# All of one float64 weight matrix narrowed beside the first batch's spectra, and the second batch's last spectra ordered behind routing steps

## Chip, cores and metric

The kernel runs on one core of a Trainium2 chip. The metric is device time in microseconds (us) of one execution; lower is better. The engines are TensorE (PE, matrix products; PEld is its load of stationary weights), VectorE (DVE), ScalarE (ACT), GpSimdE (POOL) and SyncE (SP, which issues most DMAs). Each engine takes its instructions strictly in the order in which the program was built, so an instruction that waits holds up everything behind it on that engine.

## What is computed

The reference has three steps on x of shape (4, 3072, 256), cut here to its core:

```python
X = np.fft.rfft(x, axis=1)
Yr = Xr @ w_r - Xi @ w_i + b_r
Yi = Xr @ w_i + Xi @ w_r + b_i
Yr, Yi = soft_threshold(Yr, 0.01), soft_threshold(Yi, 0.01)
x = np.fft.irfft(Yr + 1j * Yi, n=3072, axis=1).reshape(12288, 256)
logits = x @ w_gate                                     # 8 experts
each token: its best expert, gate weight = softmax there;
the first 384 tokens of each expert are kept
out = gate_w * (relu(x_kept @ w1[e]) @ w2[e]),  0 for the others
h = out @ w_in                                          # 256 x 2048
result = (h * sigmoid(h)) @ w_out                       # 2048 x 256
```

The matrices w_in and w_out of the last step come as float64. A program on this chip has no float64 arithmetic, so the kernel reads their bits as pairs of int32 and makes float32 of them with shifts and masks; this is called narrowing here.

## The kernel before

The kernel keeps float32 accuracy on PE by splitting each operand into a high and a low part and multiplying three times: mm3 (L205, L206, L207) is high x high, high x low and low x high. The high part is a copy into the rounded type by ACT (L189), the low part is the difference, by DVE or POOL (L197).

The kernel needs only the tokens that are kept, and goes on until all experts are full; for these inputs the first two of the four batches do nearly all of it. In the order of time the program does this:

1. `first` (L365): x of batch 0 is fetched in nine transfers on SP (L379, the last is `loads[8]`) and multiplied by a DFT table, in eight strips m with two halves c. Each product of a half goes to one PSUM tile ps of a pool with three buffers; half 0 is evicted to xs by ACT and half 1 by DVE (L387).
2. `kphase(0)` (L410), the spectra of batch 0: for k = 0, 2, ... 22 it turns xs (L428), finishes the DFT (xp, L436), multiplies by the weights (yp, shrink, eight times mm3, so 24 matmuls for a group), thresholds on DVE (L476 to L479, the step tail or y, then cl), and goes back (bp, L485), which ACT evicts to bo (L189) and writes to DRAM as b_d (L488). Beside it run `s1(1)` (L390), the first step of batch 1, `load_tables` (L305) and `ffn_in(0, 4)`.
3. `kphase(1)`, the same for batch 1; it reads ar from DRAM (L420). Beside it: `is2(0)`, which reads b_d back as br (L634), finishes the inverse transform (ps by L361), turns it (tp, L648) and makes the logits (lg, L661; turned back as lt, L668), and `ffn_in(4, 8)`.
4. `route(0)` (L681): the place of each token by running sums on DVE, a sum over the partitions on PE (bs, L695 to L698), one-hot matrices pm (L738 to L741), and the table of the kept tokens (tb, 24 matmuls, L753); then `rank` and `slots` (L767 to L815, DVE and POOL), which give the row numbers srcs.
5. `experts` (L919): for each expert nine rows' blocks are gathered for the first three experts by POOL's indirect DMAs (xg, L1046, three for an expert), scaled (DVE, L1057), turned (gtp, L1064), split to xT, and go through the first product (hp), relu (hh on ACT, hl on DVE) and the second (y). The weights come in quarters st on SP and are split on ACT and on DVE or POOL (w, L189 and L197). Beside experts 0 to 2 run `third(1)` (L560; reads br, L575, L589, L597, L602), `route(1)` and the second `slots`. From the point E in the order of the experts on, `second_ffn` does the last step for pairs of experts; `pair` (L1099) makes the sums t1, t2, m1 to m4 of two experts' results that it multiplies.

One part of w_in (`ffn_part`, L877) is 128 rows x 512 columns of float64. Its narrowing (`narrow`, L853) is one DMA of 512 KB into nt on SP (L861), |high word| on ACT (na, L867), and on DVE a clamp (L868), the sign (nsg, L872) and two shifts (L873, L874). Each part is then split into the weight wi by ACT and POOL; every second part also makes sums mt on DVE (L904 to L907), which are stored (L909). w_out goes the same way in `ffn_out`, one part at each step n in the list AHEAD, all behind routing.

What sets the order: the generators are stepped in turn by `mix`, with the weights of its list; the pools' buffers give the waits; and `self.after(a, b)` keeps a behind b when the instructions are put in order, without a wait at run time. The scheduler then lines up each engine's instructions by its own reckoning of when the data is there. `narrow` puts its DMA behind `self.fetched`, which is the last load of x at first and is moved forward by `kphase`. The DMAs that SP and ACT issue go to the same 16 DMA engines.

## Time and profile before

| | us |
|---|---|
| three runs | 622.52, 624.06, 628.26 |
| median | 624.06 |
| the profiled execution, as timed | 625.83 |
| its span in the trace | 624.0 |
| PE busy in it | 601.4 |
| DVE / ACT / POOL busy | 419.7 / 339.8 / 202.7 |

The profile is of one execution, and its durations are set against that execution's own 625.83 us. Busy means that the engine had an instruction in work; PE's ends are modelled, so overlapping matmuls look longer (0.28 us) than the distance at which they start. In a timeline row the first number is the start in us from the beginning of the span, the second how long the row lasted, then engine, line, operation, what it wrote and read, and how many; the bracket gives the idle time of the engine ahead of it and what ended that.

### The profile page before, as it was taken

Reading aid. Unit: us, or ns where it says so; the run is one execution under the profiler, and the core shown is the slowest. Engines: PE = TensorE matmul, PEld = TensorE weight load, DVE = VectorE, ACT = ScalarE, POOL = GpSimd, SP = SyncE. Lnnn points to the kernel's source line nnn. Section 1 sums busy time; section 2 is a strip of 40 time slices with the busy share of each in tenths; the row PEclk is TensorE's granted clock in tenths of the full one; section 3 lists DMA queues with packets and bytes.
Section 4 is the critical chain, followed back from the end, with each engine's and each line's share of the span. In section 5 each row is a group of like instructions: output and inputs, shape, how many; then the busy total and the mean of one; then the engine's idle time right before and its main releaser. Section 6 shows DMA issues by size and latency. Waiting matters only on the chain. (4 is left out here: it accounts for less than half of the span.)

```text
span 624.0 us, 11502 instructions
## 1 busy us (share of the span) xinstructions
PE 601.4 (96%) x4128; PEld 560.0 (90%) x4128; DVE 419.7 (67%) x837; ACT 339.8 (54%) x722; POOL 202.7 (32%) x196
## 2 busy tenths in 40 slices
PE   9999999799997998999999999999999999999994
PEld 9887898557996778989999999999999999999994
DVE  2454887545884669999876687576587567485563
ACT  2535555343453556457765657556557555465552
POOL 1000113300025324355754503445403343154433
PEclk9999999899998999999999999999999999999998
DMA  8638867894427777810453543413443130010001
GB/s 213 191 94 251 280 207 233 232 270 111 169 80 238 203 226 251 285 53 26 141 186 116 151 135 111 155 32 119 138 128 105 57 128 27 13 65 27 15 3 55
DMA packets 66011, 86.09 MB, mean 138 GB/s; under 512 B 6068, under 2 KB 55864, under 8 KB 65944
## 3 DMA queue, kind: packets, MB, share of 16 engines
q1 hardware_dynamic: 53976, 69.53, 37.1%
q10 hardware_dynamic: 9664, 9.44, 4.9%
q0 software_dynamic: 2304, 6.29, 3.1%
q8 instruction: 34, 0.56, 0.4%
q14 instruction: 33, 0.27, 0.1%
HBM read 54.31 MB, written 30.93 MB: 137 GB/s over the span
## 5 line engine op out<-in xcount | busy, mean ns | idle before, releaser
L1235 DVE TENSOR_TENSOR u<-h,u 128x384 f32<-128x384 f32 x224 | 117.6, 552 | 57.0 <-PE h L207 51.9
L1158 ACT ACTIVATE u<-u 128x384 f32<-128x384 f32 x128 | 64.2, 522 | 71.0 <-DVE u L1235 70.4
L206 PE MATMUL o<-wo,gl 128*128 128x256 f32 x366 | 98.8, 282 | 0.6 <-DVE gl L197 0.6
L207 PE MATMUL o<-wo,gh 128*128 128x256 f32 x366 | 98.9, 282 | 0.0
L205 PE MATMUL o<-wo,gh 128*128 128x256 f32 x366 | 86.8, 282 | 0.1
L197 POOL TENSOR_TENSOR ring<-mt,ring 128x384 fp32r<-128x384 f32 x32 | 37.9, 1186 | 129.4 <-ACT ring L189 129.4
L197 POOL TENSOR_TENSOR gl<-u,gh 128x384 fp32r<-128x384 f32 x62 | 65.1, 1068 | 29.1 <-ACT gh L189 26.4
L206 PEld LDWEIGHTS o<-wo,gl 128*128 128x128 f32 x366 | 69.2, 189 | 1.2 <-DVE gl L197 0.9
L207 PEld LDWEIGHTS o<-wo,gh 128*128 128x128 f32 x366 | 69.0, 189 | 0.0
L189 ACT CAST gh<-u 128x384 fp32r<-128x384 f32 x126 | 63.3, 510 | 5.3 <-PE o L207 3.7
L205 PEld LDWEIGHTS o<-wo,gh 128*128 128x128 f32 x366 | 64.6, 189 | 0.4 <-ACT gh L189 0.4
L205 PE MATMUL yp<-wri,xk 128*128 128x256 f32 x188 | 56.6, 301 | 0.9 <-DVE tail L476 0.9
L1086 ACT ACTIVATE hh<-hp 128x384 fp32r<-128x384 f32 x64 | 31.4, 491 | 46.6 <-PE y L206 23.6
L1087 DVE SCALAR_TENSOR_TENSOR hl<-hp,hh 128x384 fp32r<-128x384 f32 x64 | 35.1, 552 | 29.8 <-ACT hh L1086 26.0
L206 PE MATMUL yp<-wri,xk 128*128 128x256 f32 x188 | 54.5, 290 | 0.0
L207 PE MATMUL yp<-wri,xk 128*128 128x256 f32 x188 | 54.3, 289 | 0.0
L197 DVE TENSOR_TENSOR w<-st,w 128x512 fp32r<-128x512 f32 x52 | 38.1, 741 | 19.2 <-ACT w L189 18.4
L189 ACT CAST w<-st 128x512 fp32r<-128x512 f32 x64 | 38.7, 619 | 16.5 <-DMA st<-in_moe_w 8.9
L205 PE MATMUL hp<-xT,w 128*128 128x384 f32 x128 | 44.1, 345 | 1.6 <-DVE xT L197 1.6
L197 POOL TENSOR_TENSOR wi<-na,wi 128x256 fp32r<-128x256 f32 (+1 forms) x8 | 11.4, 1425 | 100.1 <-ACT wi L189 100.1
L205 PE MATMUL y<-hh,w 128*128 128x384 f32 x128 | 43.5, 340 | 0.0
L206 PE MATMUL hp<-xT,w 128*128 128x384 f32 x128 | 43.4, 339 | 0.0
(254 smaller groups left out, 1544.7 us busy)
## 6 DMA issues: line engine op xcount, KB each, us to landing
st<-in_moe_w SPq DMA_DIRECT2D x64, 256.0 KB, 3.1
out<-zt SPq DMA_DIRECT2D x48, 256.0 KB, 3.2
b_d<-bo ACTq DMA_DIRECT2D x12, 512.0 KB, 4.4
mt<-mixed SPq DMA_DIRECT2D x32, 192.0 KB, 2.4
xt<-in_x SPq DMA_DIRECT2D x15, 384.0 KB, 6.8
nt<-in_moe_w_in SPq DMA_DIRECT2D x8, 512.0 KB, 5.3
nt<-in_moe_w_out SPq DMA_DIRECT2D x16, 256.0 KB, 5.5
a_d<-ao SPq DMA_DIRECT2D x8, 384.0 KB, 4.2
```

The source lines that it names most:

```text
L189: self.lastact = self.nc.scalar.copy(dst, src)
L197: return e.tensor_tensor(dst, src, raw(hi), ALU.subtract).ins
L205: first = nc.tensor.matmul(out, lh, rh, start=start, stop=False)
L206: nc.tensor.matmul(out, ll, rh, start=False, stop=False)
L207: return first.ins, nc.tensor.matmul(out, lh, rl, start=False, stop=stop).ins
L1086: self.rectified = nc.scalar.activation(hh, hp, AF.Relu).ins
L1087: self.evicted = nc.vector.scalar_tensor_tensor(hl, hp, 0.0, raw(hh), ALU.max, ALU.subtract).ins
L1158: act.activation(sg, sg, AF.Silu)
L1235: v.tensor_tensor(to, h, u, ALU.add)
```

## The change

- `ffn_in` takes all eight parts of w_in in the first mix (with the first spectra), with no steps of delay, and none beside the second spectra. Parts 0 and 1 are put right behind the ninth transfer of x (`loads[8]`); the others stay behind `fetched`.
- HOLD: the shrinks of batch 1 for k = 10, 14 and 18 are held behind the last lt of `is2(0)`, the last bs of `route(0)` and the last tb.
- AHEAD, the steps at which parts of w_out are narrowed, goes from 4, 8, 12, 16, 20 to 7, 10, 13, 16, 20.
- `third(1)` starts four steps later and takes 5 + 2n instead of 2 + 2n steps between its parts; its first matmul of each tile is put behind `lasty`, the last product y of an expert that stands before it.
- The low half of the first quarter of expert 0's w2 goes from POOL to DVE.
- `pair`: its tiles m1 to m4 and b2 move from the pool mb to mg, the tiles gh and gl of `second_ffn` from mg to mb, and the first pair's sums are put behind the one-hot matrix of `route(1)` (`self.made`).

The diff, cut to the lines around its edits:

```diff
@@ -35,11 +35,12 @@
 WARM = 11
-AHEAD = 4, 8, 12, 16, 20
+AHEAD = 7, 10, 13, 16, 20
 PMS = "vav"
...
 PACE = {4: 2, 5: 5, **{n: GT - 1 for n in range(6, 12)}}
+HOLD = {10: "lt", 14: "bs", 18: "tb"}
 BIG = 65536.0
@@ -172,6 +173,7 @@
         self.again, self.away, self.evicted, self.gated = False, False, None, {}
+        self.held, self.lasty = {}, None
 
@@ -258,12 +260,13 @@
                 next(g)
-            mix([tables, spectra, self.s1(1, ads), self.ffn_in(0, 4)], [4, 10, 24, 10], lead=[0, 0, 0, 0])
+            mix([tables, spectra, self.s1(1, ads), self.ffn_in(0, 8, 0)], [4, 10, 24, 8], lead=[0, 0, 0, 0])
             rest = self.kphase(1, ads, True)
...
                 self.route_consts()
-            mix([self.is2(0, (0, 1, 2), self.res), self.ffn_in(4, 8)], [10, 7])
+            for _ in self.is2(0, (0, 1, 2), self.res):
+                pass
             self.route(0, (0, 1, 2), self.res)
@@ -470,7 +473,9 @@
                             l = [xk[:, h, 2 * j + c, 64 - 64 * jj:192 - 64 * jj] for h in range(2)]
-                        self.mm3(yp[:, j], l[0], l[1], wri[:, jj, 0, c], wri[:, jj, 1, c], jj + c == 0, jj + c == 2)
+                        ins = self.mm3(yp[:, j], l[0], l[1], wri[:, jj, 0, c], wri[:, jj, 1, c], jj + c == 0, jj + c == 2)[0]
+                        if b == 1 and k in HOLD and not jj and not c:
+                            self.after(ins, self.held[HOLD[k]])
             y = self.spare(1, "y")
@@ -572,7 +577,9 @@
                     u = 2 * w + z
-                    nc.tensor.matmul(pt[u * QB:(u + 1) * QB], c4, br[:, z], start=True, stop=True)
+                    ins = nc.tensor.matmul(pt[u * QB:(u + 1) * QB], c4, br[:, z], start=True, stop=True).ins
+                    if b == 1 and not u:
+                        self.after(ins, self.lasty)
             ao = bp.tile([P, 2, 2, P], F32, tag="ao", name="ao2")
@@ -665,7 +672,7 @@
                 for y in range(GS):
-                    nc.tensor.transpose(lt[:, y].rearrange("p b e -> p (b e)"), ls[:n, y], self.ident[:n, :n])
+                    self.held["lt"] = nc.tensor.transpose(lt[:, y].rearrange("p b e -> p (b e)"), ls[:n, y], self.ident[:n, :n]).ins
                 self.choose(lt.rearrange("p g b e -> p b g e")[:, :, :, :E], res[b], slice(g + 1 - GS, g + 1))
@@ -695,7 +702,7 @@
             nc.tensor.matmul(bs[:, 0, :, j:], ones, last[:, :, :NB - j], start=False, stop=j == NB - 1)
-        nc.tensor.matmul(bs[:, 1], ones, last, start=True, stop=True)
+        self.held["bs"] = nc.tensor.matmul(bs[:, 1], ones, last, start=True, stop=True).ins
         v.tensor_tensor(inc, inc, oh, ALU.mult)
@@ -750,7 +757,7 @@
             for t in range(GT):
-                nc.tensor.matmul(tb, pm[:, t], ft[:, j * GT + t], start=(j + t == 0), stop=(j * GT + t == NC - 1))
+                self.held["tb"] = nc.tensor.matmul(tb, pm[:, t], ft[:, j * GT + t], start=(j + t == 0), stop=(j * GT + t == NC - 1)).ins
         for j in range(NB):
@@ -850,7 +857,7 @@
 
-    def narrow(self, src, n, after):
+    def narrow(self, src, n, after, behind=None):
 
@@ -859,7 +866,7 @@
             ins = nc.sync.dma_start(out=t[:, dv], in_=sv.bitcast(I32).rearrange("p (n z) -> p n z", z=2))
-            self.after(ins.ins, self.fetched)
+            self.after(ins.ins, behind or self.fetched)
         low, high = t[:, :, 0], t[:, :, 1].bitcast(F32)
@@ -874,24 +881,24 @@
 
-    def ffn_part(self, src, after):
+    def ffn_part(self, src, after, behind=None):
         W = 512
         if self.i["moe2_w_in"].dtype == mybir.dt.int64:
-            return self.narrow(src, W, after)
+            return self.narrow(src, W, after, behind)
         a = self.mn.tile([P, W], F32, tag="na", name="na")
...
 
-    def ffn_in(self, q0, q1):
+    def ffn_in(self, q0, q1, late=LATE):
 
...
         nc, g = self.nc, self.nc.vector
-        for _ in range(LATE):
+        for _ in range(late):
             yield
...
             h, z = q % 2, (q // 2) * W
-            a = self.ffn_part([(self.i["moe2_w_in"][h * P:(h + 1) * P, z:z + W], slice(0, W))], None if self.again else self.shrunk)
+            a = self.ffn_part([(self.i["moe2_w_in"][h * P:(h + 1) * P, z:z + W], slice(0, W))], None if self.again else self.shrunk, None if self.again or q > 1 else self.loads[8])
             a = a.rearrange("p (i f m) -> p i f m", f=2, m=P)
@@ -937,8 +944,9 @@
             with self.stream("b", 2, "left"):
+                yield 4
                 for n, _ in enumerate(self.third(1, self.res)):
-                    yield 2 + 2 * n
+                    yield 5 + 2 * n
                 tiny = self.mc.tile([P, 1], F32, name="tiny")
@@ -970,7 +978,7 @@
                     pass
-                pre = self.pair()
+                pre = self.pair(None if again else self.made)
             part = self.first_ffn(ph, xs.pop(ph), ws[ph][0]) if ph < E else self.second_ffn(ph - E, pre)
@@ -1030,7 +1038,7 @@
                     self.after(self.lastact.ins, behind)
-                self.lo("p" if m and s < EARLY and not self.again else "v", w[:, 1], st, w[:, 0])
+                self.lo("p" if m and 0 < s + z and s < EARLY and not self.again else "v", w[:, 1], st, w[:, 0])
                 out[m].append(w)
@@ -1096,9 +1104,9 @@
 
-    def pair(self):
-
-        v, mg, mb = self.nc.vector, self.mg, self.mb
+    def pair(self, behind=None):
+
+        v, mg = self.nc.vector, self.mg
         (e, a), (_, b) = sorted(self.ys.items())[:2]
@@ -1107,12 +1115,14 @@
         def cut(nm, src):
-            t = mb.tile([P, 2, CAP], FR, name=nm, bufs=1)
+            t = mg.tile([P, 2, CAP], FR, name=nm, bufs=1)
             self.split("av", t[:, 0], t[:, 1], src)
...
         t1, t2 = (mg.tile([P, CAP], F32, tag="sg", name="tm") for _ in range(2))
-        v.tensor_tensor(t1, b[:, 0], a[:, 0], ALU.subtract)
+        ins = v.tensor_tensor(t1, b[:, 0], a[:, 0], ALU.subtract)
+        if behind:
+            self.after(ins.ins, behind)
         v.tensor_tensor(t2, b[:, 1], t1, ALU.subtract)
@@ -1120,7 +1130,10 @@
         m4 = cut("m4", a[:, 1])
-        return [*out, cut("b2", b[:, 1]), m1, m2, m3, m4]
+        b2 = cut("b2", b[:, 1])
+        if behind:
+            self.after(self.lastact.ins, behind)
+        return [*out, b2, m1, m2, m3, m4]
 
@@ -1160,7 +1173,7 @@
             else:
-                gh, gl = (mp.tile([P, CAP], FR, tag=nm, name=nm, bufs=4) for nm in ("gh", "gl"))
+                gh, gl = (self.mb.tile([P, CAP], FR, tag=nm, name=nm, bufs=4) for nm in ("gh", "gl"))
             self.hi("a", gh, sg)
```

Three places of the built order show what moves. First SP at the start, from the load of the bias on. Before:

```order
L325 DMA tail<-in_ind 2x256
L328 DMA bf<-in_b_r 1x256
L329 DMA bf<-in_b_i 1x256
L305 DMA c_225<-in_tab 128x768
L305 DMA c_226<-in_inv 128x896
L401 DMA xt<-in_x 96x1024 x3
```

and now:

```order
L328 DMA tail<-in_ind 2x256
L331 DMA bf<-in_b_r 1x256
L332 DMA bf<-in_b_i 1x256
L868 DMA nt<-in_moe_w_in 128x1024 x2
L308 DMA c_225<-in_tab 128x768
L308 DMA c_226<-in_inv 128x896
L404 DMA xt<-in_x 96x1024 x3
```

The two parts nt (L868 now) stand ahead of the second table and the inverse table.

DVE over the evictions of x's strips (`xs<-ps`, one for each strip m), before:

```order
L387 COPY xs<-ps_149 128x96x4
L387 COPY xs<-ps_163 128x96x4
L387 COPY xs<-ps_177 128x96x4
L387 COPY xs<-ps_191 128x96x4
L387 COPY xs<-ps_205 128x96x4
L387 COPY xs<-ps_219 128x96x4
L326 CAST ind<-tail 2x256
L197 TENSOR_TENSOR wri<-wf,wri 128x512 x2
```

and now:

```order
L390 COPY xs<-ps_149 128x96x4
L390 COPY xs<-ps_163 128x96x4
L390 COPY xs<-ps_177 128x96x4
L879 TENSOR_SCALAR nsg<-nt 128x512
L390 COPY xs<-ps_191 128x96x4
L390 COPY xs<-ps_205 128x96x4
L390 COPY xs<-ps_219 128x96x4
L329 CAST ind<-tail 2x256
L199 TENSOR_TENSOR wri<-wf,wri 128x512 x2
```

The sign step of the first part (`nsg<-nt`) stands between the fifth and the sixth eviction. On ACT, which has the other eight evictions, the steps `na<-nt` of the two parts now stand before the last two:

```order
L390 COPY xs<-ps_171 128x96x4
L390 COPY xs<-ps_185 128x96x4
L874 ACTIVATE na<-nt 128x512
L390 COPY xs<-ps_199 128x96x4
L874 ACTIVATE na<-nt 128x512
L390 COPY xs<-ps_213 128x96x4
L432 COPY ar<-at 128x512
```

PE behind the routing table, from the end of the spectra to the first matmul of the first expert (`hp`), before:

```order
L205 MATMUL yp<-wri,xk 128x256
L206 MATMUL yp<-wri,xk 128x256
L207 MATMUL yp<-wri,xk 128x256
L485 MATMUL bp<-cl,c_226 128x256 x2
L1064 MATMUL gtp<-ident,xg 128x128 x4
L485 MATMUL bp<-cl,c_226 128x256 x2
L1064 MATMUL gtp<-ident,xg 128x128 x2
L485 MATMUL bp<-cl,c_226 128x256 x2
L205 MATMUL hp<-xT,w_2161 128x384
```

and now:

```order
L209 MATMUL yp<-wri,xk 128x256
L207 MATMUL yp<-wri,xk 128x256
L208 MATMUL yp<-wri,xk 128x256
L209 MATMUL yp<-wri,xk 128x256
L207 MATMUL yp<-wri,xk 128x256
L208 MATMUL yp<-wri,xk 128x256
L209 MATMUL yp<-wri,xk 128x256
L490 MATMUL bp<-cl,c_226 128x256 x2
L1072 MATMUL gtp<-ident,xg 128x128 x2
L490 MATMUL bp<-cl,c_226 128x256 x2
L207 MATMUL hp<-xT,w_2161 128x384
L208 MATMUL hp<-xT,w_2161 128x384
```

Before, a whole stretch of yp ended ahead of the turns gtp of the gathered rows, and only two bp stood among the turns; now yp of the last held group stands between them. From tb to hp there are 47 matmuls of yp before and 72 now, and four and five rows bp, of which the last ones stand around hp.

## Rows read from the trace of the kernel before

**Rows 1.** The page: busy us by engine; busy tenths of PE in 40 slices.

```profile
PE 601.4 (96%) x4128; PEld 560.0 (90%) x4128; DVE 419.7 (67%) x837; ACT 339.8 (54%) x722; POOL 202.7 (32%) x196
...
PE   9999999799997998999999999999999999999994
```

**Rows 2.** Table by stretches: length; busy PE, PEld, DVE, ACT, POOL; clock, DMA share, GB/s.

```profile
16.00:24.00 8.00, 7.57 (x67) 7.18 (x66) 3.10 (x6) 3.77 (x8) 0.00 (x0) 1.00 1.04 310
88.00:96.00 8.00, 8.00 (x66) 7.86 (x65) 4.32 (x8) 2.59 (x6) 0.00 (x0) 1.00 1.02 344
96.00:104.00 8.00, 7.23 (x53) 6.65 (x52) 6.58 (x14) 5.05 (x12) 1.12 (x1) 1.00 0.46 160
104.00:112.00 8.00, 7.12 (x54) 6.56 (x53) 7.97 (x16) 5.16 (x11) 4.20 (x3) 1.00 0.93 301
112.00:120.00 8.00, 5.59 (x33) 4.35 (x33) 5.73 (x12) 2.50 (x5) 5.64 (x3) 0.91 0.81 211
120.00:128.00 8.00, 8.00 (x45) 4.39 (x44) 2.87 (x7) 2.61 (x5) 0.39 (x1) 0.88 0.83 227
184.00:192.00 8.00, 5.52 (x37) 4.41 (x35) 4.68 (x8) 3.00 (x5) 6.45 (x7) 1.00 0.90 281
192.00:200.00 8.00, 6.99 (x27) 6.22 (x28) 3.52 (x6) 3.33 (x7) 3.83 (x5) 0.79 0.62 194
216.00:248.00 32.00, 29.59 (x182) 23.32 (x180) 24.42 (x49) 18.26 (x37) 9.81 (x8) 1.00 0.78 234
248.00:284.00 36.00, 33.83 (x202) 31.96 (x203) 34.57 (x82) 19.86 (x43) 15.49 (x15) 1.00 0.52 165
```

**Rows 3.** Timeline of 14 to 24, all engines.

```profile
15.80 0.36 SPq L305 DMA_DIRECT2D c<-in_tab  x1
...
18.64 0.56 DVE L387 COPY xs<-ps 128x384 f32<-128x384 f32 x1 [1.23 <-PE ps L383]
...
20.43 0.56 DVE L387 COPY xs<-ps 128x384 f32<-128x384 f32 x1 [1.23 <-PE ps L383]
...
21.04 1.31 PE L428 MATMUL at<-ident,xs 128*128 128x128 f32 x10 [0.43 <-DVE xs L387]
```

**Rows 4.** DMA issues of 14 to 30, KB each, us to landing.

```profile
c<-in_tab SPq DMA_DIRECT2D x1, 384.0 KB, 6.8
```

**Rows 5.** DMA issues of the page, whole run, KB each, median us to landing.

```profile
b_d<-bo ACTq DMA_DIRECT2D x12, 512.0 KB, 4.4
...
nt<-in_moe_w_in SPq DMA_DIRECT2D x8, 512.0 KB, 5.3
```

**Rows 6.** Timelines of DVE, ACT, SP and PE, 92 to 130.

```profile
97.35 0.43 DVE L872 TENSOR_SCALAR nsg<-nt 128x512 int32<-128x512 int32 x1 [2.13 <-DMA nt<-in_moe_w_in]
...
107.07 1.40 DVE L907 TENSOR_TENSOR mt<-na,mt 128x256 f32<-128x256 f32 x1
...
106.01 0.37 ACTq L488 DMA_DIRECT2D b_d<-bo  x1
...
113.62 2.95 SPq L634 DMA_DIRECT2D br<-b_d  x6
...
116.82 1.07 PE L361 MATMUL ps<-br,c 48*64 48x512 f32 x4 [2.41 <-DMA br<-b_d]
```

**Rows 7.** Timelines of PE, DVE and POOL, 176 to 200.

```profile
177.61 2.76 PE L753 MATMUL tb<-ft,pm 128*128 128x72 f32 x24
...
186.78 1.03 PE L485 MATMUL bp<-cl,c 128*128 128x256 f32 x4
...
194.78 0.88 PE L205 MATMUL hp<-xT,w 128*128 128x384 f32 x1
...
188.92 0.35 DVE L1057 TENSOR_SCALAR xg<-xg,gws 128x256 f32<-128x256 f32 x1 [0.60 <-DMA xg<-attn,srcs]
...
190.65 2.05 DVE L1057 TENSOR_SCALAR xg<-xg,gws 128x256 f32<-128x256 f32 x1 [1.04 <-DMA xg<-attn,srcs]
...
191.27 1.27 POOL L197 TENSOR_TENSOR w<-st,w 128x512 fp32r<-128x512 f32 x1
```

## Prediction

> **What bounds the kernel now.** I read the page's busy shares first: the reader is to see that PE is busy 601.4 of 624.0 us [rows 1], so that the end moves only by what PE starts or stops waiting for, or by its clock. The busy tenths in 40 slices (15.6 us each) come next: below 9 stand the eighth, the thirteenth and the sixteenth, which are 109 to 125, 187 to 203 and 234 to 250, and the last, the end; between 250 and the end every slice is at 9, so that little is to be had there [rows 1]. The table by stretches gives it in microseconds: 96 to 120 has PE idle for 0.77, 0.88 and 2.41, 184 to 200 for 2.48 and 1.01, 216 to 284 for 2.41 and 2.17 [rows 2]. A clock of 0.91 and then 0.88 over 8 us each is (0.09 + 0.12) x 8 = 1.7 us of full speed lost behind the first of these, 0.79 in 192 to 200 is 1.7 again behind the second [rows 2]. Last I read the timelines of those places, for what ended each wait [rows 6, 7]. The change touches these, and one place where PE hardly waits today: the start.
>
> **A. Two parts of the first float64 matrix right behind x: a loss.** In the new order two loads nt of 512 KB stand on SP ahead of the second table, and on in-order DVE the step that reads the first of them (nsg) stands between the fifth and the sixth of its eight evictions xs; ACT has one such step before each of its last two. These evictions end no sooner than nt has landed. The first nt takes the place that the second table (384 KB) has now: issued 15.80, 6.8 us to landing, 22.6 [rows 3, 4]. The queue is full there, 310 GB/s with a share of 1.04 [rows 2], so 128 KB more are 0.4 and another 512 KB 1.7: the first nt lands at 23.0, the second at 24.7. DVE then does nsg, 0.43 [rows 6], and the sixth eviction, 0.56 [rows 3]: 24.0. PE's tiles of this stage rotate over three buffers, so its last two groups (m = 7) wait for that eviction; a group takes 0.9, by the distance of two of DVE's evictions, 18.64 to 20.43, which holds two [rows 3]. They end at 25.8, and DVE's last eviction at 26.4 (ACT's, behind the second nt, is done at 26.0 if its two steps take as long as DVE's, so no later). Now the last one ends at 20.99 and the transposes follow at 21.04 [rows 3]: +5.4, taken as +5.5 with PE's restart. Nothing covers it, since the transposes need all strips. What is moved behind the two loads (tables, three strips of x) is later too, by 1024 KB or 3.4 us, less than the transposes: no second wait. PE stands for 5 us before that, and shorter waits of 2 to 3 us were twice followed by the 1.7 us of clock: +1.2 for that (7 in 10). Bounds of A: 3.5, if nt takes from 15.80 only the page's median of 5.3 [rows 5], with no loss of clock; and 9.5, if the clock stays at half from 24 to 32.
>
> The Trainium skill speaks to this queue ("DMA: Bandwidth & Descriptors", section "Queues, rings and completion order"): each DMA engine consumes descriptors in ring order, while a later transfer's data may be complete before an earlier one's. By its first half nt comes behind the weights and x, and the 6.8 us of the table in this place [rows 4] agree; by its second half nt might overtake them in part, and A would be nearer 3.5.
>
> **B. Four parts more beside the first spectra (24 to 96).** What they bring DVE shows where they run now: busy 6.58 + 7.97 + 5.73 in 96 to 120, where three stretches like 88 to 96 would hold 3 x 4.32, so 7.3 us more. In 88 to 96 the spectra leave DVE half idle, 4.32 of 8 us, while PE doesn't wait: 8.00 [rows 2]. That slack hides them, unless a part's data is late: then in-order DVE stands as at 97.35 (2.13 us), which is what PE's idle 0.77 of 96 to 104 came from [rows 2, 6]. I take one such event, +0.8. Bounds: 0, and 3.1 for one in each of four parts.
>
> A rule against this part is in the Trainium skill, "SBUF — State Buffer": DVE and GpSimd share a port pair as an exclusive lock, and the loser blocks for the whole instruction of the other. The trace has cases that look like it: DVE's sum mt of 256 columns took 1.40 at 107.07 [rows 6], and xg 2.05 instead of 0.35 while POOL had w [rows 7]. If each of the four low parts that POOL does here cost DVE 1.0, with no slack to take it, B would be +4.0.
>
> **C. No narrowing beside the second spectra (97 to 122).** PE's idle there is 0.77 + 0.88 + 2.41 = 4.06 [rows 2]. The first two come from ACT and DVE, which were behind with narrowing steps, and go. The third is L361 at 116.82, which waits for br, read at 113.62 once the last b_d, issued at 106.01, had landed: 7.6 us, behind two nt and an ar, where the page's median for b_d is 4.4 [rows 5, 6]; I take 5.5 in a queue without nt. After: 0.8 sooner by the first wait, 0.5 by ACT's casts that stand before the eviction bo today (an estimate), so issued at 104.7 and landed at 110.2, and L361 3.2 later, as now: 113.4, which is 3.4 sooner. One product bp (1.03 long, 0.9 to the next start [rows 7]) that now stands before L361 comes behind it in the new order: 2.5 remains. PE waits there for about 1.6 instead of 2.41, and I count 0.6 of the 1.7 us of clock as kept: -1.0. C = -3.5; bounds -1.0 (b_d as slow as now) and -5.8 (4.06 and all the clock).
>
> **D. Spectra held behind routing (155 to 200).** From the end of tb (177.61 + 2.76 = 180.4) to the first hp (194.78) pass 14.4 us [rows 7]. PE does in them 47 matmuls of yp at 0.12 (66 in 8 us, [rows 2]), 5.6 us, four bp (0.9 each) and six turns gtp (taken as one bp): 10.1. So 4.3 are lost, 3.5 of it idle [rows 2], the rest restarts and low clock. The change holds three groups, k = 10, 14 and 18, behind lt, bs and tb: 72 matmuls (8.6 us) and five bp follow tb, four of these before hp: 8.6 + 3.6 + 0.9 = 13.1 of cover. The chain beside it, rank, slots (DVE), gathers (POOL), xg, gtp, has 14.4 now, in which POOL's w at 191.27 stands before the last three gathers and DVE's xg beside it took 2.05 instead of 0.35 [rows 7]; in the new order w stands behind all nine gathers, so 12.7. Cover and chain are nearly equal: I leave 0.5 of the 4.3 for chance, and 0.3 for ACT, on which steps of the second matrix's parts wait for data in the same stretch. Of the 1.7 of clock about 1.2 lies behind hp's start (194.78 to 197), and 1.0 of that goes. D = -3.8 + 0.3 - 1.0 = -4.5. Bounds: -1.5 (only POOL's step helps) and -6.0.
>
> **F. Third, second route, pair (200 to 284).** PE is idle for 2.41 + 2.17 = 4.6 [rows 2]. Third(1) starts later and is spread wider, which gives its reads more time; pair's sums run as soon as route's pm is made; a quarter of one w goes from POOL to DVE, 0.7 us where DVE has slack. But the last b_d of batch 1 comes behind hp now, so the first read of third may be late. I take a little under half, -1.8; bounds -3.9 and +0.7.
>
> **Sum.** 5.5 + 1.2 + 0.8 - 3.5 - 4.5 - 1.8 = -2.3. The profiled execution took 625.83 (span 624.0, 1.8 around it), so 623.5; the median of the three runs is 624.06, 1.8 below it, so **621.8**. A measurement of this kernel tells about 1%, 6.2 us, from no change: 617.8 and 630.3 are the edges.
>
> **Rivals.**
> 1. The start is cheap. nt lands near 21.1 and the clock stays (A 3.5), B is 0, C -4.5, D -5.8, F -2.5: -9.3, 614.8. For it: the median of 5.3 for nt [rows 5]. Against it: the full queue [rows 2].
> 2. Slower: in-order DVE and ACT become the bound, because every step that reads a part stands ahead of evictions that PE needs. Price: 9.5 at the start with the clock at half, 0.77 for each of six further parts, 4.6; the routing chain on DVE, its steps behind waiting ones, then gives D only -2.5, C -3.0, F -0.5. Sum +8.1, 632.2. It decides from the point where nt lands 2 us later than I have (25) or four parts block. For it: 97.35 [rows 6]. Against it: DVE's half-empty stage [rows 2].
> 3. The holds only move the wait: the three groups end later, and with them their b_d and what third reads, so that PE stands there instead of at gtp. D -1.0, F +1.5, the rest as above: 5.5 + 1.2 + 0.8 - 3.5 - 1.0 + 1.5 = +4.5, 628.6. Against it: the matmuls of more than one expert lie between.
>
> **Chances.** Forecast 0.50 (617 to 627), rival 1 0.27, rival 2 0.12, rival 3 0.11. Of the forecast 0.06 lies below 617.8; with rival 1, faster is 0.33. Rival 2 and 0.02 of rival 3 are slower: 0.14. Within 1%: 0.53. The range of 8 in 10 reaches into rival 1 to 612.5 and into rivals 3 and 2 to 630.
>
> **What would show it.** A: DVE's nsg ahead of the sixth xs with idle of 5 us behind nt, the first transposes between 25 and 28, a clock below 1.00 in 24 to 32; transposes at 22 would prove me wrong. B: PE's idle in 30 to 94 below 1. C: L361 3 us sooner, counted from the transposes, with idle below 2. D: gtp's idle below 1 in all and clock 1.00 from 184 to 200; 3 us of idle at gtp, or at the first read of third, would be rival 3. F: idle below 3.5 from 200 to 284.

## The result: 0.5% slower, and the profile after

The changed kernel takes 627.2 us (median of 22 runs, 624.14 to 630.22) against 623.45 for the kernel before (22 runs, 620.67 to 628.58). The ratio is 1.0051, with a 95% interval of 1.0035 to 1.0066: a loss of some 3.2 us, where 621.8, a small gain, was forecast. The traced execution of the changed kernel took 625.62 (span 623.7), 1.6 below its median; that of the kernel before took 625.83, 2.4 over its own. The two traces, taken alone, would show no difference. They are good for where the time goes; what each part is worth is read below from the ratios of the runs.

The page of the changed kernel: busy time, tenths of PE in 40 slices, and the granted clock in tenths of full speed:

```profile
PE 603.3 (97%) x4128; PEld 560.1 (90%) x4128; DVE 421.1 (68%) x838; ACT 339.7 (54%) x722; POOL 196.6 (32%) x195
...
PE   9799998999999999999999999999999999999994
...
PEclk9699999999999999999999999999999999999998
```

Against [rows 1] the dips at 109 to 125, 187 to 203 and 234 to 250 are gone or flat, and there is a new one in the second slice, 15.6 to 31.2, with the clock at 6 tenths, and a shallow one in the seventh, 94 to 109. The same by stretches (columns as in [rows 2]):

```profile
16.00:24.00 8.00, 4.97 (x37) 4.81 (x37) 1.46 (x4) 2.19 (x4) 0.00 (x0) 0.78 1.05 369
24.00:32.00 8.00, 7.78 (x42) 7.21 (x41) 2.79 (x6) 3.96 (x9) 0.00 (x0) 0.58 0.39 106
...
96.00:104.00 8.00, 8.00 (x64) 7.78 (x63) 7.40 (x14) 4.52 (x10) 1.72 (x2) 1.00 0.87 285
104.00:112.00 8.00, 5.91 (x43) 5.15 (x43) 6.54 (x12) 3.72 (x9) 1.33 (x1) 1.00 0.53 178
112.00:120.00 8.00, 8.00 (x63) 7.52 (x62) 4.64 (x8) 3.62 (x8) 0.00 (x0) 1.00 0.59 171
120.00:128.00 8.00, 8.00 (x52) 4.92 (x51) 1.83 (x4) 2.94 (x5) 0.00 (x0) 1.00 1.00 213
184.00:192.00 8.00, 7.18 (x54) 6.51 (x53) 5.96 (x12) 3.10 (x7) 4.97 (x5) 1.00 0.91 294
192.00:200.00 8.00, 7.39 (x38) 6.17 (x37) 4.28 (x8) 4.33 (x9) 5.28 (x5) 1.00 0.45 144
216.00:248.00 32.00, 31.18 (x187) 23.20 (x186) 24.65 (x48) 17.73 (x37) 10.60 (x8) 1.00 0.74 211
248.00:284.00 36.00, 34.13 (x195) 30.97 (x196) 34.75 (x87) 21.00 (x44) 16.50 (x15) 1.00 0.57 188
```

At the start the clock lost (0.22 + 0.42) x 8 = 5.1 us, and PE stood for 3. In return PE's idle in 184 to 200 fell from 3.5 to 1.4, and the two stretches at half clock (granted 0.50) that lower the clock in [rows 2] are absent; one of these is absent from a second trace of the kernel before as well (e12). The start in the timeline:

```profile
14.91 1.98 SPq L868 DMA_DIRECT2D nt<-in_moe_w_in  x2
...
21.16 0.43 DVE L879 TENSOR_SCALAR nsg<-nt 128x512 int32<-128x512 int32 x1 [5.06 <-DMA nt<-in_moe_w_in]
21.50 1.01 DVE L390 COPY xs<-ps 128x384 f32<-128x384 f32 x2
...
22.11 3.73 PE L386 MATMUL ps<-c,xt 96*128 96x96 f32 x16 [3.03 <-DVE xs L390]
...
25.63 0.63 PE L431 MATMUL at<-ident,xs 128*128 128x128 f32 x2
...
34.66 0.36 PE L207 MATMUL yp<-wri,xk 128*128 128x256 f32 x1
```

DVE stood 5.06 us behind nt with two finished strips in PSUM; PE's last groups began at 22.11, at half the clock (3.73 us for 16 matmuls), and the first transposes came at 25.63. The place that narrowing left and the place that it moved to, PE and then DVE and POOL, 100 to 124:

```profile
105.17 0.38 PE L208 MATMUL yp<-wri,xk 128*128 128x256 f32 x1 [0.86 <-DVE xk L456]
109.39 0.39 PE L208 MATMUL yp<-wri,xo 128*128 128x256 f32 x1 [1.23 <-DVE xo L199]
121.05 1.07 PE L364 MATMUL ps<-br,c 48*64 48x512 f32 x4
...
101.34 0.97 DVE L483 TENSOR_SCALAR cl<-tail 128x512 f32<-128x512 f32 x1
102.34 1.11 DVE L484 TENSOR_TENSOR cl<-tail,cl 128x512 f32<-128x512 f32 x1
...
106.57 1.49 DVE L483 TENSOR_SCALAR cl<-tail 128x512 f32<-128x512 f32 x1
...
106.45 1.33 POOL L199 TENSOR_TENSOR wi<-na,wi 128x512 fp32r<-128x512 f32 x1 [3.54 <-ACT wi L191]
```

The wait of 2.41 at the first matmul of `is2` ([rows 6]; L364 now) is gone, the row has no bracket. In its stead PE waited twice for DVE, 2.09 in all, for xk and xo of the second spectra. DVE was late with the last narrowing steps: from 100.1 to 110.2 it had no pause. Three of its steps cl were longer beside POOL's low parts wi, which lay in 101.19 to 102.91 and 106.45 to 107.78: L483 took 0.97 and 1.49, where it takes 0.42 at 96.16, and L484 took 1.11, where it takes 0.69 at 96.61. That is 2.0 us together. Behind tb:

```profile
174.90 2.85 PE L760 MATMUL tb<-ft,pm 128*128 128x72 f32 x24
...
187.83 0.44 PE L1072 MATMUL gtp<-ident,xg 128*128 128x128 f32 x2 [0.66 <-DVE xg L1065]
...
190.92 0.35 DVE L1065 TENSOR_SCALAR xg<-xg,gws 128x256 f32<-128x256 f32 x1 [0.16 <-DMA xg<-attn,srcs]
...
193.20 1.13 PE L490 MATMUL bp<-cl,c 128*128 128x256 f32 x4 [0.46 <-ACT bo L191]
193.98 0.53 PE L207 MATMUL hp<-xT,w 128*128 128x384 f32 x1
```

PE waits for turns of gathered rows once, 0.66, where [rows 2, 7] had 3.5 idle, and xg takes 0.35 where one took 2.05.

To compare stretches with unlike work in them, I count as wait what a stretch takes beyond its matmuls at the median spacing of their kind and beyond half of its time at half clock:

| stretch | before: wait / clock | changed: wait / clock | difference | forecast |
|---|---|---|---|---|
| start to first yp | 1.3 / 0 | 3.2 / 5.2 | +7.1 | A +6.7 |
| first yp to is2's first matmul | 5.0 / 0 | 3.1 / 0 | -1.9 | |
| from there to tb | 2.5 / 1.7 | 2.0 / 0 | -2.2 | with the row above B + C -2.7 |
| end of tb to first hp, and the clock behind it | 4.3 / 1.7 | 1.9 / 0 | -4.1 | D -4.5 |
| first hp to the last step's first matmul o | 5.2 / - | 6.5 / 0 | +1.3 | F -1.8 |
| from there to the end | 5.1 / 0 | 4.3 / 0 | -0.8 | 0 |

They sum to -0.6 for these two executions, whose spans differ by -0.3. The count takes half of all time at half clock as lost, PE's idle in it too, so at the start it gives some of the wait to the clock; e9 below tells the two apart.

### The profile page after: what moved, and what is told of

The parts are those of the page before. It is cut to its first block, busy times and chain, and to the rows that moved or that the text cites. A ratio compares the mean times of both kernels' runs of the same rounds, so it can differ in the third digit from the quotient of the medians.

```text
span 623.7 us, 11495 instructions
## 1 busy us (share of the span) xinstructions
PE 603.3 (97%) x4128; PEld 560.1 (90%) x4128; DVE 421.1 (68%) x838; ACT 339.7 (54%) x722; POOL 196.6 (32%) x195
## 5 line engine op out<-in xcount | busy, mean ns | idle before, releaser
L199 POOL TENSOR_TENSOR gl<-u,gh 128x384 fp32r<-128x384 f32 x62 | 65.5, 1073 | 29.8 <-ACT gh L191 25.3
L207 PE MATMUL yp<-wri,xk 128*128 128x256 f32 x188 | 56.1, 298 | 0.0
L208 PE MATMUL yp<-wri,xk 128*128 128x256 f32 x188 | 53.7, 286 | 1.0 <-DVE xk L456 1.0
L209 PE MATMUL yp<-wri,xk 128*128 128x256 f32 x188 | 53.5, 285 | 0.0
L207 PE MATMUL hp<-xT,w 128*128 128x384 f32 x128 | 43.5, 341 | 0.1
L208 PE MATMUL hp<-xT,w 128*128 128x384 f32 x128 | 43.1, 336 | 0.1
L209 PE MATMUL hp<-xT,w 128*128 128x384 f32 x128 | 42.9, 337 | 0.1
```

The source lines that it names most:

```text
L199: return e.tensor_tensor(dst, src, raw(hi), ALU.subtract).ins
L207: first = nc.tensor.matmul(out, lh, rh, start=start, stop=False)
L208: nc.tensor.matmul(out, ll, rh, start=False, stop=False)
L209: return first.ins, nc.tensor.matmul(out, lh, rl, start=False, stop=stop).ins
```

## Experiments

Each was timed against the kernel before on the same chip; ratios are to that. e1 to e8 ran on one chip and e9 to e12 on another, so what is said between the two groups goes by two ratios. The difference of two ratios is known to some 2 us. "Changed" is the changed kernel at 1.0051.

### e1: the changed kernel without the early pair

```diff
-            a = self.ffn_part([(self.i["moe2_w_in"][h * P:(h + 1) * P, z:z + W], slice(0, W))], None if self.again else self.shrunk, None if self.again or q > 1 else self.loads[8])
+            a = self.ffn_part([(self.i["moe2_w_in"][h * P:(h + 1) * P, z:z + W], slice(0, W))], None if self.again else self.shrunk, None)
```

> The changed kernel, with parts 0 and 1 of w_in put behind the later loads like the others, so that no narrowing step stands among the evictions of x's strips. Theory 1 (the loss sits at the start: evictions behind nt, then half the clock, about 7 us together in the trace, the first yp at 34.7 instead of 27.7): the first yp is back near 28 and the time is 5 to 7 us below the changed kernel, 620 to 622, about 0.5% faster than before. Theory 2 (what is lost at the start is slack that would be waited out later, and the narrowing beside the first spectra is the cost): the start is quick but PE waits 3 us or more between 30 and 120, and the time stays at 625 to 628.

620.38 us (6 runs), ratio 0.9930 (0.9905 to 0.9956). The start, 16 to 32:

```profile
16.00:24.00 8.00, 7.57 (x67) 7.18 (x67) 3.19 (x7) 3.77 (x9) 0.00 (x0) 1.00 0.97 308
24.00:32.00 8.00, 7.73 (x64) 7.23 (x62) 4.10 (x8) 5.13 (x14) 0.00 (x0) 1.00 0.44 118
```

It is as before ([rows 2]) and the first yp comes at 27.4. PE's waits between the first yp and is2 are no larger than in the changed kernel (2.6 against 3.1). So theory 1 holds: on this base the early pair alone costs 1.0051 - 0.9930, 1.2% or 7.5 us (uncertain by some 2), and without it the change is a gain of 0.7% on the kernel before.

### e2: the early loads kept, their steps behind the evictions

```diff
+        self.lastxs = dict(self.ended)
...
+        last = nc.scalar.activation(a, high, AF.Abs, scale=UP)
+        if behind:
+            self.after(last.ins, self.lastxs[0])
...
+        if behind:
+            self.after(sign.ins, self.lastxs[1])
+            self.after(first.ins, self.lastxs[1])
```

> The changed kernel, with the two early loads kept where they are, but the narrowing steps on ACT and DVE ordered behind the last evictions of x's strips. It tells the place of the loads in the DMA queue from the place of the steps on the engines. Theory 1a (in-order engines behind nt are the cost): no idle of 3 us at the strips; ACT's two steps still stand before the eviction of the first transposes, so some 2 us of wait remain there, perhaps with part of the clock; 622 to 624. Theory 1b (the queue is the cost: tables and x strips come later): the first yp stays near 33 to 35 and the time at 626 to 628.

622.54 us (12 runs), 0.9962 (0.9936 to 0.9987), 0.9% below the changed kernel. ACT's two steps now stand before the eviction ar, and PE waits for that:

```profile
20.51 1.31 PE L432 MATMUL at<-ident,xs 128*128 128x128 f32 x10 [0.43 <-DVE xs L390]
23.71 2.11 PE L440 MATMUL xp<-c,ar 128*128 128x128 f32 x12 [1.89 <-ACT ar L433]
```

The loads have the same place in the queue as in the changed kernel, yet the transposes come on time. 1a holds: the cost is the place of the steps on in-order engines, not of the loads in the queue. What is left against e1, 0.3%, is not clear of noise; the trace has for it the 1.89 us and one short stretch of half clock behind them (0.79 in 24 to 32).

### e3: the kernel before with nothing but the early pair

```diff
-            mix([tables, spectra, self.s1(1, ads), self.ffn_in(0, 4)], [4, 10, 24, 10], lead=[0, 0, 0, 0])
+            mix([tables, spectra, self.s1(1, ads), self.ffn_in(0, 4, 0)], [4, 10, 24, 10], lead=[0, 0, 0, 0])
...
-            self.after(ins.ins, self.fetched)
+            self.after(ins.ins, behind or self.fetched)
```

(`behind` is `loads[8]` for the parts 0 and 1 and nothing for the others.)

> The kernel before, with nothing changed but the early pair: four parts beside the first spectra as before, of which 0 and 1 stand right behind x. Theory 1: it loses what the start loses, 6 to 8 us, 630 to 631. Theory 2 (slack later): within 2 us of before.

629.1 us (6 runs), 1.0072 (1.0049 to 1.0096): 4.5 us slower, less than forecast by theory 1 and more than by theory 2. Its start loses as much as the changed kernel's (first yp at 34.0), but a part comes back: the wait between the first yp and is2 is 3.1 instead of 5.0. That two parts are done earlier may be why; it was not tested (a second trace of the kernel before, e12, has 4.1 there).

### e8 and e9: the changed kernel with PE kept busy while it stands

```diff
+                if m == 7 and not c:
+                    fill = self.pk.tile([P, 2, D], F32, tag="bp", name="pf", bufs=1)
+                    for z in range(FILL):
+                        dummy = nc.tensor.matmul(fill[:, 0, :P], self.zt[:, 0, :P], self.zt[:, 0, :P], start=z == 0, stop=z == FILL - 1).ins
+                        self.after(dummy, prior)
```

FILL is 30 in e8 and 14 in e9; the strip's own matmuls are put behind the last of them.

> The changed kernel with 30 matmuls on zeros (128x128 float32, into the tile of bp, which is empty then) put before PE's last two groups of x's strips, where it stands for some 3 us; they add no result. It tells the wait from the clock. Theory 1 in full (wait 2 to 3 us, and 5 us of half clock because PE stood): the clock stays at 1.00 in 20 to 31, the wait stays, and the time falls by 3 to 5 us to 622 to 624. If the clock falls anyway, or the wait is all there is, it stays at 626 to 628.

> e8 again with 14 filling matmuls instead of 30. In e8 the clock did stay up (0.996 as mean, none below 1.00 at the start), but the filler took 6.9 us in 18.6 to 25.3 (I had sized it by half its true duration), 3.2 us more than the evictions needed (22.1), and so ate what the clock gave. 14 of them are 3.2 us, 18.6 to 21.8, just short of 22.1. If the loss of the start is a wait of 2 to 3 us and 5 us of clock, the time falls by 3 to 5 us against the changed kernel, to about 0.999 to 1.000 of before; if it stays at 1.004 or more, the clock was no part of the loss.

e8 took 628.31 us, 1.0051 (1.0028 to 1.0074), no gain; e9 623.01 us, 0.9993 (0.9972 to 1.0015). The filler of e8, then e9's filler, last strip and first yp, and e9's stretches 16 to 24 and 24 to 32:

```profile
18.55 6.89 PE L389 MATMUL pf<-zt 128*128 128x128 f32 x60
```

```profile
18.29 3.32 PE L389 MATMUL pf<-zt 128*128 128x128 f32 x28
...
21.63 2.02 PE L392 MATMUL ps<-c,xt 96*128 96x96 f32 x16
...
30.94 0.37 PE L208 MATMUL yp<-wri,xk 128*128 128x256 f32 x1
```

```profile
16.00:24.00 8.00, 7.85 (x68) 7.42 (x67) 1.66 (x4) 2.49 (x5) 0.00 (x0) 1.00 1.05 366
24.00:32.00 8.00, 7.43 (x59) 6.78 (x60) 3.85 (x9) 6.24 (x15) 0.00 (x0) 1.00 0.37 94
```

In e8 my filler was too long: each of its matmuls shows as two in the trace (60 for 30), and it held PE until 25.3, 3 us more than the evictions needed. In e9 it fits: DVE waits for nt as long (5.2 against 5.06), the clock stays at 1.00, the groups of the last strip take 2.02 instead of 3.73, the first yp comes at 30.94 instead of 34.66, and the time falls by 0.6%, 3.6 us (uncertain by some 2). So of the 7.5 us of the early pair about half is the clock, and the wait is the rest: the first yp of e9 still comes 3.3 us later than that of the kernel before (27.68). The Trainium skill ("TensorE: Matmul & The Clock Gate", Part 1) says that PE falls to 1.2 GHz when it has been idle and returns to 2.4 when it has been busy. The trace agrees, and shows that to have resumed is not enough: in the changed kernel the clock stayed at half until 30.7, 8.6 us after PE had resumed at 22.11.

### e4 and e5: without the holds

```diff
-HOLD = {10: "lt", 14: "bs", 18: "tb"}
+HOLD = {}
```

> The changed kernel without the three holds, all else as changed. If the holds are worth what PE's wait before the first expert fell by (3.5 of idle and 1.7 of clock before, 1.4 and none after), it is 3 to 5 us slower than the changed kernel, 630 to 632. If the gain there came from POOL's step that left the gathers, or the held groups only move the wait, it stays within 1 us of 627.

> The kernel of e1 without the three holds. In e4 the holds made no measurable difference (1.0035 against 1.0051), but e4 had the slow start under it. If the holds gain before the first expert (PE's wait there 1.9 with them and 2.9 without, and no low clock behind it) and lose as much up to the first matmul of the last step (wait 6.5 to 8.2 with them, 4.6 without), it stays within 1.5 us of e1, 619 to 622. If the holds are worth what was forecast for them, it is 3 us or more slower, above 623.

e4 (the changed kernel): 626.07 us, 1.0035 (1.0012 to 1.0059), not slower than with the holds. e5 (e1): 620.74 us, 0.9937 (0.9913 to 0.9960) against 0.9930. On either base the holds make no difference that can be measured. Before hp they do what they should, but little of it: e4 has PE waiting there,

```profile
191.87 0.59 PE L1072 MATMUL gtp<-ident,xg 128*128 128x128 f32 x2 [2.17 <-DVE tail L481]
```

and the wait from tb to hp is 2.9 in e4 and 2.7 in e5, 1.9 in the changed kernel and in e1. So most of the fall from 4.3 comes without the holds, with the other edits. (e4 has also 1.7 of lost clock behind that wait, e5 none.) From hp to the first o the same count gives 4.6 and 6.6 without the holds, 6.5 and 8.2 with them: by the count, what they gain before the first expert is lost behind it. In what form is open, since PE's idle there does not differ as much: 2.6 in the changed kernel against 2.9 in e4, 4.1 in e1 against 3.6 in e5. Third's waits for b_d explain only a part. e1 has three of them, and then, without the holds, e5 has one:

```profile
198.94 1.05 PE L580 MATMUL ps<-br,c 96*32 96x512 f32 x4 [0.61 <-DMA br<-b_d]
...
200.55 1.05 PE L580 MATMUL ps<-br,c 96*32 96x512 f32 x4 [0.56 <-DMA br<-b_d]
...
216.55 1.05 PE L580 MATMUL ps<-br,c 96*32 96x512 f32 x4 [1.15 <-DMA br<-b_d]
```

```profile
216.47 1.05 PE L580 MATMUL ps<-br,c 96*32 96x512 f32 x4 [2.26 <-DMA br<-b_d]
```

The first two of e1, 1.2 us, have no counterpart in e5; with the third they come to as much as e5's one. The changed kernel has 0.34 of such waits, e4 1.5.

### e6 and e11: the holds with third where it was

e6 is the kernel before with the holds (the lines of the change on `held` and HOLD, nothing else). e11 is e1 with third's old steps:

```diff
-                yield 4
...
-                    yield 5 + 2 * n
+                    yield 2 + 2 * n
...
-                    if b == 1 and not u:
-                        self.after(ins, self.lasty)
```

> The kernel before with the three holds and nothing else of the change. Forecast's reason (PE needs cover behind tb): 4 to 5 us faster than before, 619. Rival 3 (the wait only moves): within 1.5 us of before, with PE's wait before the first expert smaller and the waits of third and the pair larger.

> The kernel of e1 (which has the holds) with third(1) back on its old steps: no four steps of delay, 2 + 2n instead of 5 + 2n, no order behind lasty. e6, the holds on the kernel before, was 1.3% slower, with 12.6 us of wait from the first expert to the last step's first matmul where before has 5.2. If that comes from third reading b_d of the held spectra too early, this one loses 5 us or more against e1, 1.000 to 1.006. If it came from something else in before (narrowing beside routing, pair's pools), it stays within 2 us of e1.

e6 took 631.8 us (6 runs), 1.0131 (1.0092 to 1.0170): the holds alone lose 8 us. e11 took 623.02 us, 0.9975 (0.9951 to 0.9999), 2.8 us more than e1. PE in e6 and then in e11:

```profile
202.52 1.05 PE L579 MATMUL ps<-br,c 96*32 96x512 f32 x4 [1.99 <-DMA br<-b_d]
...
246.86 0.44 PE L207 MATMUL y<-hh,w 128*128 128x384 f32 x1 [2.13 <-ACT hh L1090]
...
263.45 0.62 PE L209 MATMUL y<-hl,w 128*128 128x384 f32 x2 [2.19 <-DVE hl L1091]
```

```profile
201.35 1.05 PE L580 MATMUL ps<-br,c 96*32 96x512 f32 x4 [1.40 <-DMA br<-b_d]
...
243.53 0.44 PE L207 MATMUL y<-hh,w 128*128 128x384 f32 x1 [2.23 <-ACT hh L1091]
...
247.85 0.44 PE L207 MATMUL hp<-xT,w 128*128 128x384 f32 x1 [1.50 <-DVE xT L199]
```

Both have the same pattern: third's first read waits for the b_d of the held spectra, and later ACT and DVE are behind for the second and third expert; 12.6 and 12.0 of wait from hp to the first o, where the kernel before has 5.2 by the same count. e6 has 3.4 of lost clock there as well. With third on its early steps the holds thus lose on the kernel before, and on e1's base third's later start pays about 3 us (uncertain by 2). How much of that it pays without the holds was not run, and why e6 loses 5 us more than e11 is not told apart here (e6 also keeps the second narrowing and the old pools).

### e7: all eight parts early, nothing else

```diff
-            mix([tables, spectra, self.s1(1, ads), self.ffn_in(0, 4)], [4, 10, 24, 10], lead=[0, 0, 0, 0])
+            mix([tables, spectra, self.s1(1, ads), self.ffn_in(0, 8, 0)], [4, 10, 24, 8], lead=[0, 0, 0, 0])
...
-            mix([self.is2(0, (0, 1, 2), self.res), self.ffn_in(4, 8)], [10, 7])
+            for _ in self.is2(0, (0, 1, 2), self.res):
+                pass
```

> The kernel before with all eight parts of w_in beside the first spectra, none of them ahead of the later loads, and no other edit. By the terms of the forecast it gains C, 3.5 us, less what the parts cost beside the first spectra (0 to 0.8), so 620 to 621. If the first spectra pay for it, no gain: 623 to 625.

623.24 us (12 runs), 0.9972 (0.9950 to 0.9993): a gain of 1.7 us (0.4 to 3.1) where 2.7 was forecast. e5 is e7 with the edits to third, pair, AHEAD and w on top; the step from 0.9972 to 0.9937 is theirs, 2.2 us with an uncertainty of about 2.

### e10: w's low quarter on POOL again

```diff
-                self.lo("p" if m and 0 < s + z and s < EARLY and not self.again else "v", w[:, 1], st, w[:, 0])
+                self.lo("p" if m and s < EARLY and not self.again else "v", w[:, 1], st, w[:, 0])
```

> The kernel of e1 with the first low quarter of expert 0's w2 back on POOL, where it stands before the last three gathers again. The forecast put 1.7 us of the routing chain down to it (xg 2.05 instead of 0.35 beside it). If that holds, PE's wait between tb and the first expert grows from 1.9 to 3 or more, and the time by 1 to 2 us against e1, 0.995 to 0.996; if PE's cover hides it, 0.993 as e1.

620.59 us (12 runs), 0.9945 (0.9924 to 0.9966) against e1's 0.9930: no difference that this measurement shows. DVE's cl and xg, POOL's w and PE's last turn of the three, of e10:

```profile
183.97 2.39 DVE L484 TENSOR_TENSOR cl<-tail,cl 128x512 f32<-128x512 f32 x1
186.28 0.34 DVE L1065 TENSOR_SCALAR xg<-xg,gws 128x256 f32<-128x256 f32 x1
...
184.49 1.31 POOL L199 TENSOR_TENSOR w<-st,w 128x512 fp32r<-128x512 f32 x1
...
186.68 0.44 PE L1072 MATMUL gtp<-ident,xg 128*128 128x128 f32 x2
```

w stands before the last three gathers again, and the collision of [rows 7] came back, on the step before xg: cl took 2.39 beside w, where it takes 0.69 at 187.72, and xg had to come behind it. PE's turn of those rows (186.68) had other work before it and did not wait. So the collision costs DVE 1.7 us, and the kernel nothing that can be measured; the wait from tb to hp is 2.7, 0.8 more than in e1, but e9, with w on DVE, has 2.6.

### e12: the kernel before once more

> The kernel before once more, unchanged, for the clocks of its single runs. The traced run of before took 625.83, 2.4 over the median of 22, and holds two stretches of half clock, 3.4 us of loss; the traced run of the changed kernel lies 1.6 below its median. If half clock after a wait comes in some runs only, the mean clock differs from run to run, the slower runs have the lower one, and most runs have fewer such stretches than the traced one; the median then lies at 623 to 624 with mean clocks of 0.992 to 0.996.

623.45 us (10 runs, 622.29 to 625.96), 0.9998. Its traced execution spans 621.5, 2.5 less than that of [rows 1], with one stretch of half clock where the other has two (1.7 us less) and 0.9 less wait up to is2. The stretch that is missing is the one behind is2. Its first matmul there, xg beside POOL's w (188.92 to 190.19), and the stretch behind is2:

```profile
115.93 1.07 PE L361 MATMUL ps<-br,c 48*64 48x512 f32 x4 [1.91 <-DMA br<-b_d]
...
188.94 1.42 DVE L1057 TENSOR_SCALAR xg<-xg,gws 128x256 f32<-128x256 f32 x1 [0.91 <-DMA xg<-attn,srcs]
```

```profile
116.00:122.00 6.00, 6.00 (x38) 3.29 (x39) 1.35 (x3) 1.69 (x3) 2.39 (x2) 1.00 1.09 293
```

So the 1.7 us of clock there, of which the forecast took 1.0 for C, are not in every execution of the unchanged kernel. The mean clocks of its single runs go from 0.987 (625.96 and 624.62 us) to 0.995 (622.49). The mean over the ten is 0.991 and that of the traced run of [rows 1] 0.992, so the expectation that most runs have fewer such stretches than the traced one does not hold. One trace of this kernel is good for the place of a wait, and for its size to some 2 us.

## Why the prediction was wrong

By the ratios of the runs the change is built up so:

| step | from, to | us | forecast |
|---|---|---|---|
| all parts early (B, C) | 1, e7 0.9972 | -1.7 | -2.7 |
| third, pair, AHEAD, w on DVE (F) | e7, e5 0.9937 | -2.2 | -1.8 |
| holds (D) | e5, e1 0.9930 | -0.4 | -4.5 |
| the early pair (A) | e1, changed 1.0051 | +7.5 | +6.7 |
| all | | +3.2 | -2.3 |

Each step is uncertain by some 2 us (the first by 1.3), so only D lies clear of its forecast.

- **The step that failed is D**, "I leave 0.5 of the 4.3 for chance": it counted nearly all that is lost between tb and hp as the gain of the holds, and nothing for what the held work costs behind hp. The runs give the holds -0.4 on e1's base (e5 to e1) and +1.0 on the other (e4 to the changed kernel). POOL's step w, which D counted too, is worth 0.9 by e10, not clear of noise, so D stays short with it. In place of the gain the traces show two things. Most of the fall of the wait from 4.3 to 1.9 came without the holds (2.9 and 2.7 are left without them), so 0.8 to 1.0 of wait is theirs, and in e4, but not in e5, 1.7 of clock. And behind hp the count is larger with the holds, by 1.9 and 1.6; what that consists of stays open, since PE's idle there does not grow as much. A clear loss by the holds shows only on the kernel before, with third on its early steps (e6): there third waits for the held b_d, and ACT and DVE are late for the second and third expert.
- **Rival 3** had 0.11. Its price for D (-1.0) is near what the runs gave and its total, 628.6, near 627.2, but in part by luck: PE does not stand at third's first read in the changed kernel, whose third starts later, and the +1.5 that it had for F came as -2.2. The forecast had named that late read under F, and left it out of D.
- **A was right in its mechanism and nearly in size**, and its two terms were wrong in opposite ways. e9 tells them apart: the first yp comes 3.3 us late by the wait, not 5.5, mainly because nt was issued 0.9 earlier (14.91) and landed at 21.16 instead of the 23.0 of the forecast; and the clock takes another 3.7 (34.66 - 30.94), not 1.2. The runs give 3.9 (e1 to e9) and 3.6 (e9 to the changed kernel). I had priced the half clock by the two stretches of [rows 2]; behind this wait it lasted 10 us. For the clock my upper bound, at half from 24 to 32, was the nearer case. Rival 1 had the landing right (21.1) and the clock wrong. e2 shows the rest of the reasoning right: the step's place on the in-order engines costs, the load's place does not.
- **B and C** came to -1.7 in the runs. L361's wait fell to nothing, not to 1.6, and DVE's lateness of 2.1 (105.17 and 109.39) took its place: the event that B counted with 0.8 came once, at the end of the narrowing, and was larger. The collisions of DVE with POOL that I weighed there are in the trace: the three steps cl beside wi lost 2.0 on a DVE without a pause, by estimate as much as PE's two waits; half of the 4.0 that it would be without DVE's slack. Moving wi away was not tried.
- **F** is near its forecast in the runs (-2.2), though in the traces the wait in this stretch did not fall. e7 and e5 differ there by 4.8 and 6.6 of wait in favour of e7, and by 3.5 of clock in favour of e5. That these edits save clock rather than wait is what the two traces suggest; it was not tested by itself.
- **POOL's w** was a weak reason for part of D. The collision is no accident of one execution: beside w, xg took 1.42 in e12, and cl 2.39 in e10. But the 1.7 us were not on PE's path in e10, and putting w back made no difference that can be measured.

## What to carry to other kernels

An instruction that waits for a load costs by what stands behind it on its engine: an early load can keep its early place in the queue if the steps that read it are ordered behind the work that PE needs (e2 against the changed kernel, 0.9%). Work that is moved into a hole as cover is not free when somebody waits for its result: ask first how much of the hole is left without it (e4, e5), and follow its output to the next reader before counting the hole as gain (e6). And price a new wait of PE with the clock behind it, which can cost as much as the wait; if the wait must stay, fill it with no more matmuls than fit (e9 against e8). A collision on an engine counts only if PE waits behind it (e10).

## What was not expected of the hardware

The half clock behind one wait lasted longer than any in the kernel before. A stretch of the changed kernel, columns as in [rows 2]:

```profile
20.50:30.70 10.20, 8.37 (x38) 7.97 (x39) 3.40 (x7) 4.38 (x9) 0.00 (x0) 0.50 0.67 205
```

It began in a wait of 3.03 us and went on for 10.2 us, through 8.37 us of busy PE. In e4 it lasted 6.8 us, where the wait was 3.5; behind 1.89 us in e2 3.4, as behind 2.41 in the kernel before; and behind 1.91 us in e12 there was none. The length does not follow from the wait alone. Nor do pauses of PE explain it: from its restart at 22.11 to 30.70 PE stood for only 0.22 us. The 42 matmuls counted in 24 to 32, where e9 has 59 and e1 64, go with the half clock itself. What decides the length stays open.
